# A recurrent-memory attention loop on one core: sums as whole-array matmuls, another order of scores and V, and an output split of 256 + 384 columns

## The chip, the cores and the metric

One core of a Trainium2 chip runs the whole program. The metric is the device time of one execution in microseconds (us); lower is better. TensorE is called PE, its weight loads PEld, VectorE DVE, ScalarE ACT, GpSimd POOL, SyncE SP.

## What is computed

Two attention blocks read the same input x (1 x 2048 x 640, bf16), and a gate mixes them:

```python
g = _sigmoid((x * gate_w).sum(-1, keepdims=True))
a = _A_ref(x, A_mem0, A_Wq, A_Wk, A_Wv, A_Wo, A_seg_len)
b = _B_ref(x, B_wqkv, B_wo)
return g * a + (1 - g) * b
```

Block B is local dilated attention and has no part in the change. Block A goes through x in 64 segments of 32 tokens, one after the other, because each segment's first 8 outputs are the next one's memory:

```python
for s in range(n_seg):
    xs = x[:, s * seg_len:(s + 1) * seg_len, :].copy()
    h = jnp.concatenate([mem, xs], axis=1)            # 8 + 32 rows
    q = jnp.einsum('btd,dhe->bhte', h, Wq)            # 32 heads of 192; k, v alike
    ...
    p = _softmax(scores, axis=-1)                     # scores masked
    o = jnp.einsum('bhqk,bhke->bhqe', p, v)
    o = jnp.einsum('bhte,hed->btd', o, Wo)
    mem = o[:, :M, :].copy()
    outs.append(o[:, M:, :])
```

## The kernel before

Block B runs first (`part_b`), then `prepass` computes, for all segments at once, the projections of eight of a segment's tokens, called z below, and puts them in `zpk_dram`. Then `part_a` runs the 64 segments, here called **rounds**, and `part_z` adds the outputs of the z tokens at the end. The change is in `part_a`, with small consequences in `weights_setup`, `tile_of`, `wo_slice`, `wo_place` and `part_z`.

**Matrices.** A round works on 32 columns: 8 memory rows and 24 of the segment's tokens, in `hT` (640 features in 5 chunks of 128, `kc` = 0 to 4). Each of Wq, Wk, Wv is 640 x 6144, cut into 4 quarters J and in each of these 3 units u of 512 columns. `project` (L768) takes one unit and one chunk: four matmuls of 32 weight columns, one per column group of the array (`tile_position=(0, 32 * j)`), with the four J side by side; such four are called a **pass**. A unit needs five passes.

**Streamed weights.** Most weights stay in SBUF. 14 tiles of 384 KB, listed in `STREAM` (L15), do not fit and come from DRAM in every round, through `get_unit` (L565) into 5 rotating buffers, on SP's queue in the order of use. The output matrix Wo is cut into a column part "oa" and a column part "ob", both in tiles of 1536 columns; before the change "oa" has 384 columns (4 chunks of Wo's rows to a tile) and "ob" 256 (6 chunks to a tile).

**A round**, in the order written out by hand for PE, ACT and DVE under `manual_schedule` (L764); the code is at L959 to L1043:

1. First projections. `m_qk(i, kcs)` is unit i // 2 of Q (i even) or K (i odd). The chunks of `hT` whose memory rows are ready are taken first: `sel("oa")` of the round before has written chunks 0 to 2. Then `sel_b` (L953, L956) fetches the memory rows of the remaining chunks, `tail` (L1048, L1052) and `store` (L1058) finish the output of the round before, and the other passes follow. `c_qk(i)` (L786) is ACT's copy out of PSUM, `t_qk` (L794) the transposes, `c_t` DVE's copies.
2. Scores of the first half of the heads, h = 0: `s_a`, `s_b` (L827, L836). HALF are matmuls on half the array's rows (64), FULL on all 128. `e_exp(0)` on ACT, `e_mask(0)` (L849) on DVE.
3. V: `m_v(u)`, copied by DVE in `c_v(u)` (L883), unit 1 in two halves. Between them stand `e_norm(h)` (L859), the sums of the exponentials as matmuls with the block diagonal of ones `bones`, four 32-column groups for each of two widths (160 and 64); `e_recip_a` (ACT: Ln, Exp), `e_recip_b` (DVE: L871, L872); and the scores and the mask of h = 1.
4. P·V: `pv_half(h)` (L899, L904) for h = 0 after three passes of V's last unit, with the other two behind `e_norm(1)`; `c_x`, `c_z` (L913, L920) copy the results on ACT and DVE.
5. Output: `o_group(part, i2)` (L942), twelve groups of four matmuls for each part; the first six of a part need the first P·V only. The order is six of "oa", `pv_half(1)`, five of "ob", six of "oa", the copy of "oa" (L1032, ACT, to `whi`), seven of "ob" with `sel("oa")` after the fourth, the copy of "ob" (L1040). ACT also issues the DMA of the round's z results (`oz_dram`, L1025) and the load of the next round's z data (`load_z`, L753).

PSUM: `psm` has two banks under one tag, taken in turn; Q's and K's units (but for K's first), V's units and the two output parts use it. `part_z` takes its accumulators from the same pool (L1101), "oa" first, and scales them on DVE (L1110).

Of the kernel before, what the change touches and what calls it, by code (L numbers as in the profile page):

```python
# [11 lines left out]
F32 = mybir.dt.float32  # L12
# [3 lines left out]
          ("v", 2, 2), ("oa", 0), ("ob", 0), ("oa", 5), ("ob", 7))  # L16
# [13 lines left out]
class _K:  # L30
# [466 lines left out]
    def weights_setup(self):  # L497
# [5 lines left out]
        rest += [k for k in [("oa", i) for i in range(12)] + [("ob", i) for i in range(8)] if k not in STREAM]  # L503
# [10 lines left out]
    def tile_of(self, pool, k):  # L514
        n = 1536 if k[0] in ("oa", "ob") else 512 * len(self.units(*k))
        t = pool.tile([128, n], BF, name="w_" + "_".join(map(str, k)))
        self.res_tiles[k] = t if n < 1536 or k[0] in ("q", "k", "v") else t[:].rearrange(
            "p (c f) -> p c f", c=4 if k[0] == "oa" else 6)
        return t
# [13 lines left out]
    def wo_slice(self, k, dst):  # L533

        n, f0, f1 = (4, 0, 384) if k[0] == "oa" else (6, 384, 640)
# [3 lines left out]
    def wo_place(self, part, c):  # L539

        n = 4 if part == "oa" else 6
# [178 lines left out]
    def part_a(self):  # L720
# [4 lines left out]
        with ctx:  # L725
# [22 lines left out]
            psm = ctx.enter_context(tc.tile_pool(name="psm", bufs=2, space=bass.MemoryType.PSUM, reuse_waits="tile"))  # L748
# [16 lines left out]
            for s in range(nseg):  # L765
                pqs, sts, pTs, pSs = {}, {}, {}, {}

                def project(ps, m, u, kcs):  # L768
                    for kc in kcs:
                        st = self.get_unit((m, u, kc)) if (m, u, kc) in STREAM else None  # L770
                        for j in range(4):
                            rhs = self.res(m, j, kc, 512 * u, 512) if st is None or j == 3 else st[:, 512 * j:512 * j + 512]
                            nc.tensor.matmul(ps[32 * j:32 * j + 32, :], lhsT=hT[:, kc, :], rhs=rhs, start=(kc == 0),  # L773
                                             stop=(kc == KC - 1), tile_position=(0, 32 * j), skip_group_check=True)
# [46 lines left out]
                def s_a(R, chunks):  # L821
# [3 lines left out]
                    for t, par, k0, k1 in chunks:  # L825
# [4 lines left out]
                                         start=(r == 0 and t == 1), stop=False, tile_position=(k0, 0),  # L830
                                         skip_group_check=True)

                def s_b(h, chunks):
                    for t, par, k0, k1 in chunks:
# [4 lines left out]
                                         start=False, stop=(t != 1), tile_position=(k0, 0), skip_group_check=True)  # L839
# [12 lines left out]
                def e_norm(h):  # L852
# [3 lines left out]
                    for x, E_x in ((80, EA), (32, EB)):  # L856
                        for j in range(4):
# [69 lines left out]
                def o_group(part, i2):  # L927
                    n = 384 if part == "oa" else 256
                    if i2 == 0:
                        pso[part] = psm.tile([128, 512], F32, tag="m", name="ps_wo")  # L930
                    for jj in range(4):
# [3 lines left out]
                        if (part, i) not in osl:  # L935
# [5 lines left out]
                            osl[part, i] = w[:].rearrange("p (c f) -> p c f", c=4 if part == "oa" else 6)  # L941
# [68 lines left out]
                m_v(2, (0, 1, 2))  # L1010
# [4 lines left out]
                m_v(2, (3, 4)); c_v(2)  # L1015
# [4 lines left out]
                for i2 in range(6):  # L1020
                    o_group("oa", i2)
# [10 lines left out]
                nc.scalar.copy(whi[:, 0:384], pso["oa"][:, 0:384])  # L1032
# [142 lines left out]
```

## Time and profile before

| | us |
|---|---|
| three runs | 1703.22, 1704.7, 1705.23 |
| median of them | 1704.7 |
| the profiled execution | 1702.23 |
| its span, first to last instruction | 1700.5 |
| first and 63rd `tail` matmuls in it | 385.4 and 1616.9 |
| matmuls of `part_z` in it | 1642.0 to 1696.4 |

In a row of the page's groups or of a timeline stand the engine, the line, the operation, what it writes and reads, the shapes and the count; "busy, mean ns of one" and the idle time of the engine just before, with what ended it in brackets. "issue" there means that no semaphore explains the wait. A timeline row begins with its start and its duration in us, and merges neighbours of one kind (x16); the duration of a matmul is that of its whole way through the array, so that successive ones overlap, and their pace is read from the starts. A row of the windows view gives the stretch, its length, the busy time (and count) of PE, PEld, DVE, ACT and POOL, the granted clock of PE, the DMA share and GB/s. PEld is the loading of weights, which runs beside the matmuls. Lines are those of the kernel before.

### The profile page before, as it was taken

The page shows a single profiled execution, that of the slowest core. Times are in us where ns is not written, and L with a number is a line of the kernel's source. Part 1 is how long each engine was busy: PE and PEld are TensorE (multiplying, and loading weights), DVE is VectorE, ACT ScalarE, POOL GpSimd, SP SyncE. Part 2 cuts the span into 40 slices and gives each one's busy share as a digit, 9 for nine tenths or more (in the row PEclk, how much of TensorE's full clock was granted, in tenths as well). Part 3 has the DMA queues.
Part 4 walks back from the last instruction along what each step waited for, and adds up shares of the span by engine and source line. Part 5 has one row for each costly group of instructions (what it writes and reads, how often), then busy time and mean ns, then how long its engine had stood idle before and what let it go on. Part 6 is the DMA issues. An engine that isn't in the chain of part 4 may idle for free.

```text
span 1700.5 us, 75713 instructions
## 1 busy us (share of the span) xinstructions
PE 1600.5 (94%) x33209; PEld 887.1 (52%) x33209; DVE 700.9 (41%) x2223; ACT 804.5 (47%) x2082; POOL 59.8 (4%) x124
## 2 busy tenths in 40 slices
PE   7887999989999999999999999999999999999989
PEld 4544544445555555555555555555555555555559
DVE  3665333234434444443344434434444434444430
ACT  3877422234444444444445444445454444454450
POOL 2030000000000000000000000000000000000000
PEclk9999899999999999999999999999999999999999
DMA  7798798889989999998999989999999999999981
GB/s 202 186 209 216 227 312 232 257 245 305 305 301 311 305 303 313 300 313 288 300 314 313 308 288 309 318 299 320 304 321 306 306 300 304 307 309 309 306 274 31
DMA packets 307608, 479.44 MB, mean 282 GB/s; under 512 B 100556, under 2 KB 186444, under 8 KB 307276
## 3 DMA queue, kind: packets, MB, share of 16 engines
q1 hardware_dynamic: 208144, 418.12, 75.8%
q10 hardware_dynamic: 99132, 56.46, 11.8%
q8 instruction: 260, 4.26, 1.0%
q14 instruction: 72, 0.59, 0.1%
HBM read 432.76 MB, written 47.23 MB: 282 GB/s over the span
## 4 chain that ended last, share of the span: by engine, by line
PE 85%; DMA 6%; ACT 3%; issue 3%; DVE 1%; SPq 1%; ACTq 0%; DVEq 0%
PE ps_qk L773 25%; PE ps_v L773 13%; PE ps_wo L942 13%; PE ps_pre L622 6%; PE ps_qkT L794 5%; PE ps_S L827 5%; PE ps_oT L899 3%; PE ps_z L1106 3%; PE ps_pre L652 3%; DMA wst<-wscr 2%; PE ps_S L859 2%; PE ps_bqk L236 2%; ACT ZB L1032 2%; DMA bqkT<-bqk_dram 1%; PE ps_mem L953 1%
## 5 line engine op out<-in xcount | busy, mean ns | idle before, releaser
L773 PEld LDWEIGHTS <-hT 128*32 128x32 bf16 x11520 | 277.2, 97 | 287.0 <-issue 18.6
L786 ACT CAST TZ<-ps_qk 128x512 bf16<-128x512 f32 x384 | 218.7, 587 | 315.3 <-PE ps_qk L773 315.3
L773 PE MATMUL ps_qk<-w_q,hT 128*32 128x512 bf16 x3264 | 267.9, 383 | 1.8 <-issue 1.6
L773 PE MATMUL ps_qk<-w_k,hT 128*32 128x512 bf16 x3264 | 266.0, 380 | 2.4 <-issue 2.0
L773 PE MATMUL ps_v<-w_v,hT 128*32 128x512 bf16 x3072 | 245.5, 384 | 0.0
L805 DVE COPY ZB<-ps_qkT 128x512 bf16<-128x512 bf16 (+1 forms) x256 | 91.0, 356 | 349.4 <-PE ps_qkT L794 253.7
L942 PEld LDWEIGHTS <-TZ 128*32 128x32 bf16 x6144 | 146.0, 96 | 110.4 <-ACT TZ L913 39.9
L883 DVE CAST TZ<-ps_v 128x512 bf16<-128x512 f32 (+1 forms) x256 | 136.9, 556 | 45.5 <-PE ps_v L773 45.5
L942 PE MATMUL ps_wo<-w_oa,TZ 128*32 128x384 bf16 x2560 | 147.4, 330 | 7.3 <-issue 6.8
L773 PE MATMUL ps_qk<-wst,hT 128*32 128x512 bf16 x1152 | 149.0, 381 | 0.8 <-DMA wst<-wscr 0.8
L913 ACT CAST TZ<-ps_oT 128x192 bf16<-128x192 f32 x256 | 75.9, 322 | 129.7 <-PE ps_oT L904 83.8
L942 PE MATMUL ps_wo<-w_ob,TZ 128*32 128x256 bf16 x2304 | 108.2, 275 | 14.0 <-issue 13.9
L956 DVE CAST hT<-ps_mem 128x24 bf16<-128x24 f32 x126 | 22.5, 179 | 227.6 <-PE ps_mem L953 227.6
L913 DVE CAST TZ<-ps_oT 128x192 bf16<-128x192 f32 x256 | 85.8, 355 | 57.7 <-PE ps_oT L904 55.8
L773 PE MATMUL ps_v<-wst,hT 128*32 128x512 bf16 x768 | 100.7, 387 | 9.0 <-DMA wst<-wscr 8.9
L794 PE MATMUL ps_qkT<-ident,TZ 128*128 128x128 bf16 x1536 | 107.3, 219 | 0.0
L794 PEld LDWEIGHTS <-TZ 128*128 128x128 bf16 x1536 | 88.6, 98 | 26.9 <-issue 26.9
L942 PE MATMUL ps_wo<-wst,TZ 128*32 128x256 bf16 (+1 forms) x1280 | 96.9, 302 | 4.8 <-issue 4.4
L845 ACT ACTIVATE TZ<-ps_S 32x224 bf16<-32x224 f32 x256 | 89.3, 349 | 13.0 <-PE ps_S L836 10.7
L845 ACT ACTIVATE ZB<-ps_S 32x224 bf16<-32x224 f32 x256 | 89.2, 348 | 13.0 <-PE ps_S L836 9.3
L754 POOL COPY TZ<-ZB 128x384 bf16<-128x384 bf16 x64 | 32.5, 507 | 1467.4 <-DMA ZB<-zpk_dram 565.1
L827 PE MATMUL ps_S<-ZB,TZ 64*128 64x160 bf16 (+1 forms) x704 | 78.1, 234 | 0.0
(135 smaller groups left out, 2037.6 us busy)
## 6 DMA issues: line engine op xcount, KB each, us to landing
wst<-wscr SPq DMA_DIRECT2D x896, 384.0 KB
zpk_dram<-ZS ACTq DMA_DIRECT2D x4, 3072.0 KB
ZB<-zpk_dram ACTq DMA_DIRECT2D x64, 192.0 KB
zpk_dram<-ZV ACTq DMA_DIRECT2D x32, 192.0 KB
TZ<-zpk_dram ACTq DMA_DIRECT2D x64, 96.0 KB
oz_dram<-TZ ACTq DMA_DIRECT2D x64, 96.0 KB
w_q<-in_A_Wq_dram SPq DMA_DIRECT2D x14, 384.0 KB
w_k<-in_A_Wk_dram SPq DMA_DIRECT2D x14, 384.0 KB
```

Of the source, the lines that this page charges most:

```text
L622: nc.tensor.matmul(ps[:], lhsT=weights(j, kc, 6 * Rp + 3 * r + t), rhs=zTi[:, kc, :], start=(kc == 0), stop=(kc == KC - 1))
L652: mm = nc.tensor.matmul(pss[g][:], lhsT=zTi[:, kc, 128 * st:128 * st + 128], rhs=weights(kc, g), start=(kc == 0), stop=(kc == KC - 1))
L773: nc.tensor.matmul(ps[32 * j:32 * j + 32, :], lhsT=hT[:, kc, :], rhs=rhs, start=(kc == 0), stop=(kc == KC - 1), tile_position=(0, 32 * j), ...
L786: nc.scalar.copy(sts[i], pqs[i][:])
L794: nc.tensor.transpose(pT[:, 128 * t:128 * t + 128], st[:, 128 * t:128 * t + 128], self.ident[:])
L805: nc.vector.tensor_copy(QTf[:, run[2]:run[2] + 4, run[3]:run[3] + n, :].rearrange("p b x i -> p x b i"), src.rearrange("p (x b i) -> p x b ...
L827: nc.tensor.matmul(grid(h, par)[:, :, 0:80].rearrange("p j (b r i) -> p j b r i", r=2, i=8)[:, :, :, r, :], lhsT=KTs[3 * R + t][k0:k1, :], ...
L845: nc.scalar.activation(E[ps], pSs[h][ps, :, 112 * j:112 * j + 112], ACT.Exp, scale=scale_a)
L883: nc.vector.tensor_copy(VU[u][:, f0:f1], pvs[u][:, f0:f1])
L899: nc.tensor.matmul(out[:, r, t, :], lhsT=Vt[6 * h + 3 * r + f0 // 128][ks, f0 % 128:f0 % 128 + f1 - f0], rhs=E[ks, par, 0:80].rearrange("p ...
L913: cp(oTxs[2 * h + j // 2][:, 6 * (j % 2):6 * (j % 2) + 6, :], pos[j][:, 0:240].rearrange("p (c q) -> p c q", q=40)[:, :, 8:40])
L942: nc.tensor.matmul(pso[part][32 * jj:32 * jj + 32, 0:n], lhsT=oTxs[2 * (g // 2) + J // 2][:, 6 * (J % 2) + 3 * (g % 2) + t, :], rhs=osl[pa ...
```

## The change

- **Output split.** "oa" becomes columns 0 to 255 (6 chunks to a tile, 8 tiles), "ob" columns 256 to 639 (4 chunks to a tile, 12 tiles). The streamed output tiles become ob 0, oa 0, oa 7 and ob 5.
- **Order of the output.** Six groups of "ob", the second P·V, all twelve of "oa", its copy (256 columns), six of "ob" with `sel("oa")` after the fourth of them, the copy of "ob" (384 columns). `sel("oa")` now brings chunks 0 and 1 of the next `hT`, `sel_b` chunks 2 to 4.
- **Order of the first projections.** Ahead of `sel_b`: chunks 0 and 1 of `m_qk(0)` and of `m_qk(1)` and chunk 0 of `m_qk(2)`; one pass of `m_qk(2)` instead of `m_qk(1)` between `sel_b` and `tail`; then chunks 2 to 4 of each. `start` and `stop` of a unit go by count, since chunks don't all come in the same order. The two `psm` banks get a tag each, so that Q's second unit can be open beside Q's first.
- **First sums.** For h = 0, `e_norm` is one matmul of the whole array for each width, two instead of eight.
- **Second scores.** For h = 1 FULL comes ahead of HALF.
- **V.** Two passes of V's last unit stand ahead of the first P·V instead of three, three behind `e_norm(1)` instead of two.

The diff, cut to its core:

```diff
 
 STREAM = (("k", 0, 2), ("q", 1, 1), ("k", 1, 2), ("q", 2, 1), ("q", 2, 4), ("k", 2, 4), ("v", 0, 0), ("v", 1, 0), ("v", 1, 3),
-          ("v", 2, 2), ("oa", 0), ("ob", 0), ("oa", 5), ("ob", 7))
+          ("v", 2, 2), ("ob", 0), ("oa", 0), ("oa", 7), ("ob", 5))
 ...
-        n, f0, f1 = (4, 0, 384) if k[0] == "oa" else (6, 384, 640)
+        n, f0, f1 = (6, 0, 256) if k[0] == "oa" else (4, 256, 640)
 ...
             for s in range(nseg):
                 pqs, sts, pTs, pSs = {}, {}, {}, {}
 
+                def bank(n, name):
+                    return psm.tile([128, 512], F32, tag="mn"[(s + n) % 2], name=name)
+
+                done = {}
+
                 def project(ps, m, u, kcs):
                     for kc in kcs:
+                        n = done[m, u] = done.get((m, u), 0) + 1
                         st = self.get_unit((m, u, kc)) if (m, u, kc) in STREAM else None
                         for j in range(4):
                             rhs = self.res(m, j, kc, 512 * u, 512) if st is None or j == 3 else st[:, 512 * j:512 * j + 512]
-                            nc.tensor.matmul(ps[32 * j:32 * j + 32, :], lhsT=hT[:, kc, :], rhs=rhs, start=(kc == 0),
-                                             stop=(kc == KC - 1), tile_position=(0, 32 * j), skip_group_check=True)
+                            nc.tensor.matmul(ps[32 * j:32 * j + 32, :], lhsT=hT[:, kc, :], rhs=rhs, start=(n == 1),
+                                             stop=(n == KC), tile_position=(0, 32 * j), skip_group_check=True)
 
                 def m_qk(i, kcs):
                     if i not in pqs:
                         pqs[i] = psS.tile([128, 2, 512], F32, tag="S", name="ps_qk")[:, 0, :] if i == 1 else \
-                            psm.tile([128, 512], F32, tag="m", name="ps_qk")
 ...
-                                         start=(r == 0 and t == 1), stop=False, tile_position=(k0, 0),
+                                         start=(r == 0 and (t == 1) == (h == 0)), stop=False, tile_position=(k0, 0),
 ...
                     pz = pSs[h][:, 0, 0:160].rearrange("p (a f) -> p a f", a=2)
                     for x, E_x in ((80, EA), (32, EB)):
+                        if h == 0:
+                            nc.tensor.matmul(pz[:, :, 0:x], lhsT=self.bones[:], rhs=E_x, start=(x == 80), stop=(x == 32))
+                            continue
 ...
-                        pvs[u] = psm.tile([128, 512], F32, tag="m", name="ps_v")
+                        pvs[u] = bank(u != 1, "ps_v")
 ...
-                    m0, m1 = (0, 3) if part == "oa" else (3, KC)
+                    m0, m1 = (0, 2) if part == "oa" else (2, KC)
 ...
-                m_qk(0, (0, 1, 2))
+                m_qk(0, (0, 1))
                 m_qk(1, (0, 1))
+                m_qk(2, (0,))
                 if sel_b is not None:
                     sel_b()
-                m_qk(1, (2,))
+                m_qk(2, (1,))
                 if tail is not None:
                     tail()
-                m_qk(0, (3, 4)); c_qk(0)
-                m_qk(1, (3, 4)); c_qk(1)
+                m_qk(0, (2, 3, 4)); c_qk(0)
+                m_qk(1, (2, 3, 4)); c_qk(1)
                 if store is not None:
                     store()
-                m_qk(2, range(KC)); c_qk(2)
+                m_qk(2, (2, 3, 4)); c_qk(2)
                 m_qk(3, range(KC)); c_qk(3)
                 m_qk(4, (0, 1))
 ...
                 e_norm(0); e_recip_a(0); e_recip_b(0)
+                s_a(2, FULL); s_a(3, FULL); s_b(1, FULL)
                 s_a(2, HALF); s_a(3, HALF); s_b(1, HALF)
-                s_a(2, FULL); s_a(3, FULL); s_b(1, FULL)
                 e_exp(1)
                 m_v(1, (1, 2, 3, 4)); c_v(1)
                 e_mask(1)
-                m_v(2, (0, 1, 2))
+                m_v(2, (0, 1))
                 pos = pv_half(0)
                 c_x(0, pos, (0, 1, 3), "add")
                 e_norm(1)
                 e_recip_a(1)
-                m_v(2, (3, 4)); c_v(2)
+                m_v(2, (2, 3, 4)); c_v(2)
                 e_recip_b(1)
                 c_x(0, pos, (2,), "a")
                 c_z(0, pos, (1, 3), "aa")
                 c_z(0, pos, (0, 2), "dd")
                 for i2 in range(6):
-                    o_group("oa", i2)
+                    o_group("ob", i2)
                 pos = pv_half(1)
                 c_x(1, pos, range(4), "adda")
                 c_z(1, pos, range(4), "adad")
                 nc.scalar.dma_start(self.oz_dram[s], zst)
                 if s + 1 == nseg:
                     self.sort_oz(0)
-                for i2 in range(5):
-                    o_group("ob", i2)
-                for i2 in range(6, 12):
+                for i2 in range(12):
                     o_group("oa", i2)
-                nc.scalar.copy(whi[:, 0:384], pso["oa"][:, 0:384])
+                nc.scalar.copy(whi[:, 0:256], pso["oa"][:, 0:256])
                 if s + 1 < nseg:
                     load_z(s + 1)
                     pm = psS.tile([128, 2, 512], F32, tag="S", name="ps_mem")
-                for i2 in range(5, 12):
+                for i2 in range(6, 12):
                     o_group("ob", i2)
-                    if i2 == 8 and s + 1 < nseg:
+                    if i2 == 9 and s + 1 < nseg:
                         sel("oa", hT_next, pm)
-                nc.scalar.copy(whi[:, 384:640], pso["ob"][:, 0:256])
+                nc.scalar.copy(whi[:, 256:640], pso["ob"][:, 0:384])
                 if s + 1 < nseg:
 ...
-            for part, f0, nf in (("oa", 0, 384), ("ob", 384, 256)):
-                ps = psm.tile([128, 512], F32, tag="m", name="ps_z")
+            for part, f0, nf in (("oa", 0, 256), ("ob", 256, 384)):
+                ps = psm.tile([128, 512], F32, tag="m" if f0 else "n", name="ps_z")
```

More of the change, by code (lines that the diff above doesn't have):

```diff
@@ L502, in weights_setup @@
             rest += [(m, J, kc) for kc in ks for J in range(4)]
-        rest += [k for k in [("oa", i) for i in range(12)] + [("ob", i) for i in range(8)] if k not in STREAM]
+        rest += [k for k in [("oa", i) for i in range(8)] + [("ob", i) for i in range(12)] if k not in STREAM]
         n = (0, N_EARLY, -N_MID - N_V - N_LAST, -N_V - N_LAST, -N_LAST, None)
@@ L517, in tile_of @@
         self.res_tiles[k] = t if n < 1536 or k[0] in ("q", "k", "v") else t[:].rearrange(
[L518 removed]
+            "p (c f) -> p c f", c=6 if k[0] == "oa" else 4)
         return t
@@ L539, in wo_place @@
     def wo_place(self, part, c):
-        n = 4 if part == "oa" else 6
+        n = 6 if part == "oa" else 4
         return c // n, c % n
@@ L778, in m_qk @@
                         pqs[i] = psS.tile([128, 2, 512], F32, tag="S", name="ps_qk")[:, 0, :] if i == 1 else \
-                            psm.tile([128, 512], F32, tag="m", name="ps_qk")
+                            bank(i == 2 or i == 4, "ps_qk")
                     project(pqs[i], ("q", "k")[i % 2], i // 2, kcs)
@@ L927, in o_group @@
                 def o_group(part, i2):
-                    n = 384 if part == "oa" else 256
+                    n = 256 if part == "oa" else 384
                     if i2 == 0:
-                        pso[part] = psm.tile([128, 512], F32, tag="m", name="ps_wo")
+                        pso[part] = bank(part == "oa", "ps_wo")
                     for jj in range(4):
```

6 lines of the change are left out of this document (3 added, 3 removed).

## The prediction

> **What bounds the kernel now.** I read the page first, then the span between two marks of the loop, then PE's waits, then one loop round in order of time. From the page, the shares of engines, the chain that ended last, and the queue that brings PE its instructions:
>
> ```profile
> PE 1600.5 (94%) x33209; PEld 887.1 (52%) x33209; DVE 700.9 (41%) x2223; ACT 804.5 (47%) x2082; POOL 59.8 (4%) x124
> PE 85%; DMA 6%; ACT 3%; issue 3%; DVE 1%; SPq 1%; ACTq 0%; DVEq 0%
> L786 ACT CAST TZ<-ps_qk 128x512 bf16<-128x512 f32 x384 | 218.7, 587 | 315.3 <-PE ps_qk L773 315.3
> q8 instruction: 260, 4.26, 1.0%
> ```
>
> PE is the bound: 94% busy, 85% of the chain. So a change pays only by what it takes out of PE's own line of work, or out of a wait that stops PE. The groups by line, cut to the stretch 385 to 1617 us and to the line of `tail`, give the length of a round (four matmuls each):
>
> ```profile
> L1048 PE MATMUL ps_a<-ZB,sel_x x252: 232/233/233, 385.4 to 1616.9; 128*32 128x160 bf16 x126
> ```
>
> 252 / 4 = 63 rounds begin between 385.4 and 1616.9, 62 intervals, 19.86 us each. One without a pause, 1064.62 to 1083.68, takes 19.06 (PE and PEld rows mixed with DVE and ACT, start, duration; an LDWEIGHTS row in brackets tells who let PE go on):
>
> ```profile
> 1064.62 0.24 PE L1048 MATMUL ps_a<-ZB,sel_x 128*32 128x160 bf16 x4
> ...
> 1073.47 0.39 PE L773 MATMUL ps_v<-wst,hT 128*32 128x512 bf16 x3
> 1073.51 0.27 DVE L849 TENSOR_TENSOR TZ<-TZ,mask 128x224 bf16<-128x224 bf16 x1 [0.19 <-ACT TZ L845]
> 1073.83 0.28 PE L859 MATMUL ps_S<-TZ,bones 128*32 128x160 bf16 x8
> 1074.05 0.24 PE L827 MATMUL ps_S<-ZB 64*128 64x160 bf16 x2
> 1074.35 0.24 PE L827 MATMUL ps_S<-ZB 128*128 128x160 bf16 x1
> 1074.43 0.30 PE L827 MATMUL ps_S<-ZB,TZ 128*128 128x160 bf16 x2
> 1074.63 0.27 PE L836 MATMUL ps_S<-ZB,TZ 128*128 128x128 bf16 x2
> 1074.84 0.61 PE L773 MATMUL ps_v<-w_v,hT 128*32 128x512 bf16 x8
> 1075.94 0.76 DVE L883 CAST TZ<-ps_v 128x256 bf16<-128x256 f32 x2 [0.62 <-PE ps_v L773]
> 1076.46 0.17 PEld L899 LDWEIGHTS <-TZ 32*128 32x128 bf16 x16 [0.42 <-DVE TZ L883]
> 1076.61 0.26 DVE L849 TENSOR_TENSOR ZB<-ZB,mask 128x224 bf16<-128x224 bf16 x1
> 1076.93 0.28 PE L859 MATMUL ps_S<-ZB,bones 128*32 128x160 bf16 x8
> 1077.04 0.60 PE L773 MATMUL ps_v<-w_v,hT 128*32 128x512 bf16 x8
> 1077.53 0.35 PE L942 MATMUL ps_wo<-wst,TZ 128*32 128x384 bf16 x4
> 1077.70 0.69 DVE L883 CAST TZ<-ps_v 128x512 bf16<-128x512 f32 x1
> 1078.80 0.17 PEld L899 LDWEIGHTS <-TZ 32*128 32x128 bf16 x16 [0.40 <-DVE ZB L872]
> 1079.27 0.40 PE L942 MATMUL ps_wo<-wst,TZ 128*32 128x256 bf16 x6
> 1080.37 0.66 PE L942 MATMUL ps_wo<-w_oa,TZ 128*32 128x384 bf16 x12
> 1080.58 0.35 ACTq L1025 DMA_DIRECT2D oz_dram<-TZ  x1
> 1080.86 0.61 PE L942 MATMUL ps_wo<-w_ob,TZ 128*32 128x256 bf16 x16
> 1081.08 0.48 ACT L1032 CAST ZB<-ps_wo 128x384 bf16<-128x384 f32 x1 [0.54 <-PE ps_wo L942]
> 1081.61 0.14 PEld L953 LDWEIGHTS <-ZB 128*128 128x128 bf16 x3 [0.43 <-ACT ZB L1032]
> 1081.78 0.39 PE L942 MATMUL ps_wo<-wst,TZ 128*32 128x256 bf16 x6
> 1081.89 0.18 DVE L956 CAST hT<-ps_mem 128x24 bf16<-128x24 f32 x1 [1.44 <-PE ps_mem L953]
> 1082.12 0.77 PEld L773 LDWEIGHTS <-hT 128*32 128x32 bf16 x20
> 1082.34 0.37 ACT L1040 CAST ZB<-ps_wo 128x256 bf16<-128x256 f32 x1 [0.78 <-PE ps_wo L942]
> 1083.32 0.11 PEld L953 LDWEIGHTS <-ZB 128*128 128x128 bf16 x2 [0.42 <-issue]
> 1083.68 0.24 PE L1048 MATMUL ps_a<-ZB,sel_x 128*32 128x160 bf16 x4
> ```
>
> Four waits of PE lie in it: for the first mask (L859, 1073.83), the V copy (1076.46), the second normalisation (1078.80) and the copy of the first output part (1081.61). The other 0.80 us of a mean round are single pauses of up to 2 us that no semaphore ends ("issue"), mostly in the output stage:
>
> ```profile
> PE ps_wo L942 <- issue: 23.9, 25, 1.9
> PE ps_qk L773 <- DMA wst<-wscr: 0.3, 1, 0.3
> 981.93 0.62 PE L942 MATMUL ps_wo<-w_ob,TZ 128*32 128x256 bf16 x16 [1.94 <-issue]
> 983.30:986.20 2.90, 2.90 (x38) 0.97 (x34) 0.17 (x1) 0.37 (x1) 0.51 (x1) 0.52 0.58 188
> ```
>
> I read them as PE's instructions coming late: 4.26 MB came in 260 packets, 16 KB each, and 2 x 33209 instructions make 64 bytes each, so 256 to a packet; the output and P·V stages use them up fastest. Streamed weights are late just once (0.3 us). The last row shows a pause's second price: after 1.94 us of idling the granted clock of the stretch 983.3 to 986.2 is 0.52, and 38 matmuls run in 2.9 us.
>
> **Prices.** A pass is four matmuls in the four column groups. Seven passes of 512 columns lie from 1074.84 to 1076.46, 1.62; with 0.09 for the change of array shape that is 0.219 a pass. Three of 384 columns: 1080.37 to 1080.86, 0.164. Three of 256: 1081.78 to 1082.12, 0.11. The change of shape: the two L836 at 1074.63 stream 2 x 128 columns, 0.11, yet the next begins at 1074.84: 0.10 left over. PE's end to a copy's start is 0.22 (1080.86 to 1081.08), a copy's end to PE 0.05.
>
> **Step 1, first sums and second scores.** Eight sums in column groups become two of the whole array; 64 x 12 PE instructions go. Before: 1073.83 to 1074.05, 0.22, of which 0.10 is the change to half arrays. The new form stands in no row. By columns 160 + 64 cost 0.10; by the nearest rows, whole-array matmuls of 160 columns from 1074.35 to 1074.43, two cost 0.16. I take 0.13. The whole-array scores follow without a change of shape, so full (0.49 with one change) and half (0.30 with one) cost as now: 0.22 becomes 0.13, **-0.09**. The new change ahead of the sums is free while the mask covers it: the last pass starts at 1073.47, its successor could at 1073.69, the mask ends at 1073.78, and the sums start at 1073.83, so 0.14 of waiting covers 0.10. If it doesn't, the step saves nothing.
>
> The Trainium skill, "TensorEngine Tiling (Array Packing)", Key Properties, says that changing the tiling mode drains TensorE, while another tile of the same mode does not. Counted by that alone the edit gains nothing, six microseconds less in the sum: three changes from one V pass to the next before, three after. The trace's 0.10 agrees that a change costs something, and its 0.14 wait is why I count one as free.
>
> **Step 2, a V pass moved behind P·V.** `m_v(1)` begins at 1074.75 and its copy 1.10 later as now, 1075.85; the first half takes about 0.42 (0.76 for two that overlap), so 1076.27, and P·V may use it at 1076.32. With six passes instead of seven PE is there at 1076.15: 0.17 of the 0.22 moved becomes a wait for DVE (P·V's first matmuls read the older V tile, but what they win ends at the next gate). DVE's second mask follows that copy, 1076.78, so the second sums go at 1076.84 (-0.09). Three passes instead of two then end at 1077.61; the V copy starts 0.22 later, at 1077.83 instead of 1077.70, and DVE's chain from it to the second P·V (1077.70 to 1078.80, 1.10) stays: 1078.93, **+0.13**. PE would be ready at 1077.61 + 0.98 + 0.10 = 1078.69, so more passes there cover nothing.
>
> **Step 3, output split.** 48 x 384 and 48 x 256 columns stay; only order and cover change. P·V ends at 1079.40 (0.47 later, as now). Twelve groups of 256 end at 1080.71 and the copy, now 256 columns (0.37), could start at 1080.93. But on ACT's queue ahead of it stands the store of oz (1080.58 to 1080.93, waiting for copies of P·V), now 0.13 later, to 1081.06. Copy 1081.08 to 1081.45, `sel` at 1081.50 instead of 1081.62. PE itself is ready at 1080.71 + 0.66 + 0.10 = 1081.47: four groups of 384 cover what four of 256 didn't. After it two matmuls and two groups of 384, 0.13 + 0.33, or the hT cast, some 0.24 + 0.18 + 0.05: projection at 1081.97 instead of 1082.12, **-0.15**.
>
> **Step 4, first projections.** Still five passes between, but `sel_b` has three matmuls: +0.03. ACT copies of 0.59 now come after 3, 6 and 9 passes (0.66 apart) instead of 2, 4 and 9; both orders put 16 passes ahead of the transposes, so nothing. SP asks for streamed units in the order of use, each when the fifth before it is released; ("q",1,1) now takes the place of ("k",0,2) and comes no later than that did. The copy of the last part is 0.48 long and must also free the bank for Q's second block at the fifth pass, 1081.97 + 0.88 = 1082.85; it ends near 1082.66, 0.2 ahead. A round: **-0.12**, times 63 = -7.
>
> **Step 5, the rest.** Pauses for instructions: 12 fewer of some 890 a round take 1% of 50 us, -0.5; the output stretch gets denser and the V stretch thinner, so 0 to me, bounds -4 to +6. Lost cover (the 0.2 for the bank when a ZB load holds ACT's queue; streamed units closer together): +1. At the end, part Z:
>
> ```profile
> 1642.70 0.47 ACT L1032 CAST ZB<-ps_wo 128x384 bf16<-128x384 f32 x1
> 1643.22 0.83 PE L1106 MATMUL ps_z<-wst,w_q 128*32 128x384 bf16 x16 [0.88 <-ACT ZB L1032]
> ```
>
> Its first bank is now freed by the second copy, not the first: +0.4. Sum: -7 - 0.5 + 1 + 0.4 = -6. The profiled execution took 1702.2 (span 1700.5 and 1.7 around it), so 1696; the runs' median is 1704.7, 2.5 above, and I forecast for the median: **1698.5**.
>
> **Rivals.**
> 1. The gain is eaten (0.20): the change of shape isn't hidden and the moved pass costs all its 0.22 at the second P·V. For: that wait is DVE's already. Against: the 0.14. A round: +0.22 at 1079.02, `sel` at 1081.59, -0.03 + 0.03 = 0; the median stays at 1704 to 1706.
> 2. The copy isn't held by the store, and the second V copy waits less (0.08): `sel` at 1081.30 to 1081.47, -0.2 to -0.3 a round, 1687 to 1692. For: engines' queues may run ahead. Against: 1080.58 + 0.35 fits closely before 1081.08.
> 3. Slower, by streamed weights (0.07). The last streamed unit of the output (the 256-column one at 1081.78) becomes a 384-column one at 1080.71 + 0.33 = 1081.04, 0.74 earlier, while its slot is free only 0.09 earlier. If units land in the last 0.65 us before their use, PE waits there: from 0.18 us a round on the kernel is slower (1708), at 0.65 it is 1739. Against: just one wait of 0.3 in 62 rounds. No row shows when a unit lands.
> 4. More instruction pauses (0.10): `sel` to the next projection has the same instructions in 0.28 less, so pauses that end there (25 now) grow by that, +7, and each that passes 2 us adds some 1.5 at half clock: 1702 to 1711.
>
> The Trainium skill, "Runtime: NRT & Kernel Launch", Instruction fetch mechanics, says that the sequencer fetches 256 instructions at a time during execution and that this is mostly hidden. By that rule rival 4 and my -0.5 would be nothing. The 1.94 us pause that no semaphore ended speaks against it here.
>
> **How the numbers follow.** Forecast (steps 1 to 4 as worked out, 1695 to 1701) 0.55; rivals as given. About 0.2%, 3.4 us, is what can be told from no change: below 1701.3 is faster, above 1708.1 slower. Faster: 0.55 + 0.08 = 0.63. Same: 0.20 and half of rival 4, 0.05, is 0.25. Slower: 0.07 and the other half is 0.12. The range, 1689 to 1707, leaves out rival 3's long part and the ends of 2 and 4.
>
> **What would show it.** In a round without pauses: 18.94 us from `tail` to `tail`; sums to scores 0.13; whole-array scores at once after them; P·V's first half stopped by L892's V copy; second P·V 0.13 later against the mask; `sel` let go by ACT, the oz store ending just before its copy; instruction pauses near 0.8 us a round. Wrong if the sums take 0.2, if DMA ends waits at the new output units, or if pauses pass 1 us a round.

## The result, and the profile after it

| | before | after |
|---|---|---|
| median of the runs, us | 1704.97 (4 runs, 1703.22 to 1711.09) | **1682.77** (4 runs, 1678.37 to 1684.86) |
| ratio after / before | | 0.9856, 95% interval 0.9829 to 0.9882 |
| the profiled execution, us | 1702.23 | 1683.8 |
| first `tail` | 385.4 | 380.2 |
| 62 rounds, first to 63rd `tail` | 1231.5 | 1216.3 |
| the shortest round | 19.06 | 18.92 |
| pauses in a mean round | 0.81 | 0.70 |
| last part, from the 63rd `tail` to the end of the span | 83.5 | 85.5 |

The kernel is faster by 1.4%, 22 us. The sign was forecast, the size was not: 1698.5 was expected, and the result lies below the range of 1689 to 1707. In this table and below, the **clean round** is the 3rd percentile of the 62 distances from one first `tail` matmul to the next (the shortest lie within 0.01 us of each other), and the pauses are the mean distance less that. So the 18.4 us between the two profiled executions are 5.2 ahead of the first `tail` (the first round is among them), 62 x 0.14 = 8.8 in clean rounds, 62 x 0.10 = 6.4 in pauses, and 2 given back from the 63rd `tail` on.

Lines shift by 6 to 9 in the changed kernel: `project` is L779, the copies of Q and K L792, the first sums L864, the scores L833 and L842, the V copy L892, P·V L908 and L913, the output L951, `sel` L962, its cast L965, the two output copies L1040 and L1048, `tail` L1056. From the page of the changed kernel, the engines, the chain, the Q and K copies and PE's instruction queue:

```profile
PE 1583.4 (94%) x32809; PEld 908.9 (54%) x32825; DVE 704.8 (42%) x2223; ACT 812.9 (48%) x2082; POOL 59.8 (4%) x124
PE 77%; DMA 10%; DVE 5%; issue 4%; ACT 2%; ACTq 1%; SPq 0%; DVEq 0%
L792 ACT CAST TZ<-ps_qk 128x512 bf16<-128x512 f32 x384 | 224.6, 585 | 309.9 <-PE ps_qk L779 299.4
q8 instruction: 257, 4.21, 1.0%
```

PE is still the bound, with 94% of a span that is 18.5 us shorter. The first and the last row belong together: by the code 64 x 6 matmuls and as many loads are gone, and 3 packets of 16 KB with them. (The counts fall by 400 and 384: this trace lacks the records of 16 matmuls of `prepass`.)

Next, one round of the changed kernel without a pause, from the timeline (start, duration, and in brackets the idle time and what ended it). It runs from `tail` at 1361.85 to `tail` at 1380.77:

```profile
1361.85 0.24 PE L1056 MATMUL ps_a<-ZB,sel_x 128*32 128x160 bf16 x4
...
1371.06 0.26 PE L864 MATMUL ps_S<-TZ,bones 128*128 128x160 bf16 x2
1371.16 0.23 PE L833 MATMUL ps_S<-ZB 128*128 128x160 bf16 x1
...
1371.64 0.10 PEld L833 LDWEIGHTS <-ZB 64*128 64x128 bf16 x2
...
1371.94 0.61 PE L779 MATMUL ps_v<-w_v,hT 128*32 128x512 bf16 x8
...
1373.04 0.76 DVE L892 CAST TZ<-ps_v 128x256 bf16<-128x256 f32 x2 [0.53 <-PE ps_v L779]
1373.35 0.27 PEld L908 LDWEIGHTS <-TZ 32*128 32x128 bf16 x16 [0.42 <-issue]
...
1373.71 0.27 DVE L855 TENSOR_TENSOR ZB<-ZB,mask 128x224 bf16<-128x224 bf16 x1
...
1374.03 0.28 PE L868 MATMUL ps_S<-ZB,bones 128*32 128x160 bf16 x8
...
1375.01 0.69 DVE L892 CAST TZ<-ps_v 128x512 bf16<-128x512 f32 x1 [0.28 <-PE ps_v L779]
...
1376.11 0.17 PEld L908 LDWEIGHTS <-TZ 32*128 32x128 bf16 x16 [0.56 <-DVE ZB L881]
...
1377.89 0.35 ACTq L1035 DMA_DIRECT2D oz_dram<-TZ  x1
...
1378.29 0.37 ACT L1040 CAST ZB<-ps_wo 128x256 bf16<-128x256 f32 x1 [0.43 <-PE ps_wo L951]
...
1378.71 0.11 PEld L962 LDWEIGHTS <-ZB 128*128 128x128 bf16 x2 [0.37 <-ACT ZB L1040]
...
1379.18 0.86 PEld L779 LDWEIGHTS <-hT 128*32 128x32 bf16 x20 [0.22 <-DVE hT L965]
...
1380.38 0.14 PEld L962 LDWEIGHTS <-ZB 128*128 128x128 bf16 x3 [0.34 <-issue]
...
1380.77 0.24 PE L1056 MATMUL ps_a<-ZB,sel_x 128*32 128x160 bf16 x4
```

To compare it with the round of before, take off the start of each (1361.85 here, 1064.62 there):

| us from `tail` | before | forecast | after |
|---|---|---|---|
| first sums | 9.21 | 9.21 | 9.21 |
| first scores behind them | 9.43 | 9.34 | 9.31 |
| V passes | 10.22 | 10.13 | 10.09 |
| first P·V | 11.84 | 11.70 | 11.50 |
| second sums | 12.31 | 12.22 | 12.18 |
| second P·V | 14.18 | 14.31 | 14.26 |
| `sel` | 16.99 | 16.88 | 16.86 |
| next projection | 17.50 | 17.35 | 17.33 |
| next `tail` | 19.06 | 18.94 | 18.92 |

This is the part of the forecast that held. What did not lies between such rounds. PE's waits, from the first `tail` to the 63rd (total us, times, longest):

```profile
PE ps_oT L908 <- DVE ZB L881: 11.1, 62, 0.2
PE ps_wo L951 <- issue: 10.7, 17, 1.3
PE ps_qk L779 <- issue: 6.4, 7, 1.9
PE ps_qk L779 <- ACT ZB L1048: 3.8, 5, 1.1
PE ps_qk L779 <- DMA wst<-wscr: 1.4, 2, 1.2
```

Before, the output's pauses, which nothing but "issue" ends, came to 23.9 us in 25 places; now it is 10.7 in 17. These rows count idle time from the moment the last matmul has left the array, so they give less than what the pace loses (the pause of 1.94 us that the prediction shows is 2.26 from start to start).

### The profile page after: what moved, and what is told of

The parts are those of the page before. It is cut to its first block, busy times and chain, and to the rows that moved or that the text cites. A ratio compares the mean times of both kernels' runs of the same rounds, so it can differ in the third digit from the quotient of the medians.

```text
span 1682.0 us, 74929 instructions
## 1 busy us (share of the span) xinstructions
PE 1583.4 (94%) x32809; PEld 908.9 (54%) x32825; DVE 704.8 (42%) x2223; ACT 812.9 (48%) x2082; POOL 59.8 (4%) x124
## 4 chain that ended last, share of the span: by engine, by line
PE 77%; DMA 10%; DVE 5%; issue 4%; ACT 2%; ACTq 1%; SPq 0%; DVEq 0%
PE ps_qk L779 25%; PE ps_v L779 11%; PE ps_wo L951 9%; PE ps_pre L622 6%; DMA wst<-wscr 5%; PE ps_qkT L800 5%; PE ps_S L833 4%; PE ps_z L1114 3%; PE ps_pre L652 3%; PE ps_oT L908 2%; DVE TZ L892 2%; DMA bqkT<-bqk_dram 2%; PE ps_bqk L236 1%; PE ps_S L842 1%; DVE ZB L880 1%
## 5 line engine op out<-in xcount | busy, mean ns | idle before, releaser
L779 PEld LDWEIGHTS <-hT 128*32 128x32 bf16 x11520 | 285.2, 96 | 299.5 <-issue 30.2
L792 ACT CAST TZ<-ps_qk 128x512 bf16<-128x512 f32 x384 | 224.6, 585 | 309.9 <-PE ps_qk L779 299.4
L779 PE MATMUL ps_qk<-w_q,hT 128*32 128x512 bf16 x3264 | 287.3, 383 | 5.6 <-ACT ZB L1048 3.8
L779 PE MATMUL ps_qk<-w_k,hT 128*32 128x512 bf16 x3264 | 252.9, 379 | 5.3 <-issue 4.9
L779 PE MATMUL ps_v<-w_v,hT 128*32 128x512 bf16 x3072 | 244.2, 384 | 0.0
L951 PEld LDWEIGHTS <-TZ 128*32 128x32 bf16 x6144 | 161.5, 96 | 52.3 <-issue 20.4
L892 DVE CAST TZ<-ps_v 128x512 bf16<-128x512 f32 (+1 forms) x256 | 136.9, 556 | 58.2 <-PE ps_v L779 58.0
L951 PE MATMUL ps_wo<-w_ob,TZ 128*32 128x384 bf16 x2560 | 153.3, 327 | 2.1 <-issue 2.0
L779 PE MATMUL ps_qk<-wst,hT 128*32 128x512 bf16 x1152 | 150.7, 382 | 1.4 <-DMA wst<-wscr 1.4
L779 PE MATMUL ps_v<-wst,hT 128*32 128x512 bf16 x768 | 101.4, 386 | 8.8 <-DMA wst<-wscr 8.8
L965 DVE CAST hT<-ps_mem 128x16 bf16<-128x16 f32 x126 | 22.5, 179 | 202.7 <-PE ps_mem L962 202.7
L951 PE MATMUL ps_wo<-w_oa,TZ 128*32 128x256 bf16 x2304 | 92.0, 273 | 7.8 <-issue 7.8
L951 PE MATMUL ps_wo<-wst,TZ 128*32 128x256 bf16 (+1 forms) x1280 | 97.1, 297 | 2.2 <-issue 2.2
L908 PEld LDWEIGHTS <-TZ 32*128 32x128 bf16 (+1 forms) x4096 | 47.1, 97 | 72.1 <-DVE ZB L881 36.1
```

Of the source, the lines that this page charges most:

```text
L792: nc.scalar.copy(sts[i], pqs[i][:])
L892: nc.vector.tensor_copy(VU[u][:, f0:f1], pvs[u][:, f0:f1])
L908: nc.tensor.matmul(out[:, r, t, :], lhsT=Vt[6 * h + 3 * r + f0 // 128][ks, f0 % 128:f0 % 128 + f1 - f0], rhs=E[ks, par, 0:80].rearrange("p ...
L951: nc.tensor.matmul(pso[part][32 * jj:32 * jj + 32, 0:n], lhsT=oTxs[2 * (g // 2) + J // 2][:, 6 * (J % 2) + 3 * (g % 2) + t, :], rhs=osl[pa ...
```

## The experiments

Two accounts were open. The first, that of the prediction: the change pays by its clean round, pauses are a toll that stays. The second: the V pass behind P·V thins out PE's instructions just where they come late, so step 2, counted as a loss, is what pays. Each kernel below was run beside the kernel before on the same chip; e1 to e4 share one, e5 to e8 another, e9 to e12 a third. "Pauses" and "clean" are as above and come from the one profiled execution of each.

### Undoing one part each

e1 puts the V pass back:

```diff
-                m_v(2, (0, 1))
+                m_v(2, (0, 1, 2))
 ...
-                m_v(2, (2, 3, 4)); c_v(2)
+                m_v(2, (3, 4)); c_v(2)
```

> The changed kernel with three V passes ahead of the first P.V again and two behind it (step 2 undone). Theory A, the schedule of PE's waits as worked out in the prediction: the moved pass costs 0.13 to 0.2 us a round, so without it the round without pauses falls from the changed kernel's 18.92 to 18.7 to 18.8 us, and the kernel is 8 to 12 us faster than the changed one if pauses stay at 0.70 us a round. Rival B, the moved pass thins PE's instructions where they are used fastest: the round without pauses falls as in A, but pauses grow to 0.9 or more a round and the time is that of the changed kernel or above.

e2 puts the first sums back into eight matmuls, and HALF ahead of FULL:

```diff
-                        if h == 0:
-                            nc.tensor.matmul(pz[:, :, 0:x], lhsT=self.bones[:], rhs=E_x, start=(x == 80), stop=(x == 32))
-                            continue
 ...
+                s_a(2, HALF); s_a(3, HALF); s_b(1, HALF)
                 s_a(2, FULL); s_a(3, FULL); s_b(1, FULL)
-                s_a(2, HALF); s_a(3, HALF); s_b(1, HALF)
```

> The changed kernel with eight sums in column groups and half-array scores first again (step 1 undone). Theory A: the round without pauses is 19.0 us instead of 18.92, so 5 to 6 us slower than the changed kernel. Rival B, fewer PE instructions mean fewer pauses: beside the 0.09, pauses go back from 0.70 to 0.80 us a round, and the kernel is 11 to 13 us slower than the changed one.

e3 has both of these edits: what is left is the output split with the first projections.

> The output split of 256 + 384 with its order and the new first projections alone; steps 1 and 2 undone. Theory A: the copy of the first part waits for PE or for ACT's oz store at 16.33 us into the round, sel starts near 16.75, and the round without pauses is 18.8 us (19.06 before, 18.92 after): with pauses as before, 0.80, the kernel is 15 us faster than before. Rival B, pauses depend on the density of PE's instructions and grow: 0.9 to 1.1 a round, and the kernel gains 5 us or less.

e4 is the changed kernel again, with no edit.

> The changed kernel unchanged, to see what differs from one execution to the next. Theory A, the part ahead of the loop (4.3 us shorter in the first profile, although its instructions are the same) and the pauses vary from execution to execution: the round without pauses is 18.92 again, the start of the loop differs by some us, pauses between 0.6 and 0.8 a round. Rival B, both belong to the change: the first tail again near 380 us and pauses at 0.70 within 0.03.

| | median us (runs) | ratio to before, 95% | clean | pauses |
|---|---|---|---|---|
| e1, V pass back | 1689.72 (12) | 0.9940, 0.9910 to 0.9970 | 18.71 | 1.01 |
| e2, sums back | 1687.76 (6) | 0.9921, 0.9892 to 0.9949 | 19.05 | 0.58 |
| e3, split alone | 1699.13 (12) | 0.9974, 0.9951 to 0.9997 | 18.84 | 0.98 |
| e4, changed again | 1682.58 (6) | 0.9885, 0.9853 to 0.9917 | 18.92 | 0.74 |

The clean rounds add up: the split takes 0.22 off (19.06 to 18.84), the sums 0.13 (18.84 to 18.71, and 19.05 to 18.92), and the moved pass adds 0.20 or 0.21 (18.71 to 18.92, 18.84 to 19.05). Yet the version with the shortest clean round, e1, is 7 us slower than e4. Its waits, then those of e2, then the largest of e3, over the 62 rounds:

```profile
PE ps_wo L951 <- issue: 32.9, 34, 1.8
PE ps_qk L779 <- issue: 3.0, 6, 1.1
```

```profile
PE ps_wo L948 <- issue: 12.1, 20, 1.2
PE ps_oT L905 <- DVE ZB L878: 11.2, 62, 0.2
```

```profile
PE ps_wo L948 <- issue: 29.6, 30, 1.9
```

With the pass ahead of P·V the output loses 32.9 us in 34 pauses (e1) and 29.6 in 30 (e3); with it behind, 12.1 in 20 (e2), 10.7 in 17 and, in e4, 14.7 in 21. In place of them stands a wait for DVE of 0.18 in each of the 62 rounds, 11.2 in all. The first account is refuted here: the moved pass costs 0.20 of a clean round and saves 0.27 to 0.40 of pauses. And the split by itself adds pauses, 0.98 against 0.81, which takes most of its 0.22 back: e3 is hardly faster than before. Undoing the sums (e2) costs 5 us against e4 and brings no pauses back.

### A second trace of the kernel before

> The kernel before, unchanged, for a second trace of it. Two readings of the 5 us by which the changed kernels reached the first tail earlier (380.2 to 382.8 us in four traces, 385.4 us in the one trace of before). If that belongs to the change, this trace has its first tail at 385 again; if it is how one execution differs from another, it lies at 381 to 383. In both: clean round (the 3rd percentile of the 62 lengths tail to tail) 19.06 us, 892 PE instructions in it, pauses 0.75 to 0.9 us a round.

It took 1705.6 us in the median (12 runs; ratio to the kernel before 1.0003, 0.9977 to 1.0030), clean round 19.06, pauses 0.83. Its first `tail` and the largest wait:

```profile
L1048 PE MATMUL ps_a<-ZB,sel_x x252: 232/233/233, 383.4 to 1616.4; 128*32 128x160 bf16 x126
PE ps_wo L942 <- issue: 24.2, 27, 1.6
```

So the pauses of before repeat. The first `tail` does not: 383.4 here, 385.4 in the first trace, against 380.2 to 382.8 in the five traces of e1 to e4 and the changed kernel. In later runs of versions of it, it is at 383.2 to 384.3 (e10 to e12). The two sets overlap, so I do not count the 5 us to the change but for about one: the last matmul of `prepass`, ahead of the first round, starts at 356.9 and 355.0 in the two traces of before and at 352.6 to 357.7 in those of the changed kernel and its versions, and in the first round PE then waits 5.6 and 5.3 us for a streamed tile of V before (5.1 in e9, which has the old split) and 4.2 to 4.6 with the new split.

### The same kernels without streamed weights

If the pauses are PE waiting for instructions that stand behind weights in the DMA engines, they must go when the loop streams nothing. In e6 (the kernel before), e7 (the changed one) and e8 (the changed one with the V pass back) `get_unit` returns one of five tiles loaded once, so the loop leaves the streaming out and multiplies by these five tiles where it would take the streamed ones:

```diff
         if key in self.ahead:
-            return self.ahead.pop(key)
+            return self.ahead[key]
+        if len(self.ahead) == WBUFS:
+            return self.ahead[STREAM[STREAM.index(key) % WBUFS]]
```

> The kernel before, in which the loop loads no streamed weights: five tiles are loaded once and used again in turn, so projections and output multiply by wrong weights of the right size, and the queues carry about 300 GB/s less in the loop. Theory (PE's pauses come when it uses up 256 instructions faster than the next 16 KB of them arrive between the weights): the pauses fall from 0.81 to under 0.2 us a round, the clean round stays 19.06, the whole takes 1645 to 1660 us. Rival (the pauses are inside PE, whatever the queues do): 0.7 to 0.9 a round as before, 1700 us.

> The same edit to the changed kernel: no streamed weights in the loop, wrong weights in their place. Theory: pauses fall from 0.70 to under 0.2 us a round, the clean round stays 18.92, the whole 8 to 12 us under the kernel before without stream, which is what the clean round alone gives (62 x 0.14 = 8.7). Rival: pauses stay at 0.7.

> The same edit, and the V pass back ahead of P.V (step 2 undone). With the stream this version was slower than the changed kernel by 7 us, with a clean round 0.20 us shorter and pauses 0.27 to 0.3 longer. Theory (the moved pass pays only by parting the instructions, so that the fetch keeps up): without the stream the order turns over, clean round 18.71 and pauses under 0.2, and the whole is 10 to 13 us FASTER than the changed kernel without stream. Rival (the moved pass helps by something else, such as the copies' order or the exchange of PSUM banks): it stays slower by 4 to 8 us.

| | median us (6 runs each) | ratio to before, 95% | clean | pauses |
|---|---|---|---|---|
| e6, before | 1640.06 | 0.9619, 0.9584 to 0.9653 | 19.05 | 0.04 |
| e7, changed | 1633.71 | 0.9582, 0.9551 to 0.9613 | 18.88 | 0.10 |
| e8, changed, V pass back | 1619.47 | 0.9494, 0.9464 to 0.9525 | 18.67 | 0.08 |

The order turns over: with the stream the changed kernel beats the version with the pass put back by 7 us, without it that version is 14 us ahead, 62 x 0.21 = 13 of it from the clean round. Two times came out beside what was expected: e6 is 5 us under its range, and e7 is 6 us ahead of e6 instead of 8 to 12. The windows view of 600 to 1500 us for the changed kernel with the stream and then for e7 (busy us of PE, PEld, DVE, ACT and POOL, PE's clock, share of the DMA engines, GB/s), and last the waits of e6, e7 and e8 for instructions at the output, over their 62 rounds:

```profile
600.00:1500.00 900.00, 866.65 (x20134) 499.63 (x20135) 387.52 (x1380) 451.04 (x1284) 22.86 (x46) 1.00 0.94 310
```

```profile
600.00:1500.00 900.00, 887.33 (x20838) 511.53 (x20834) 397.97 (x1421) 466.75 (x1325) 24.36 (x48) 1.00 0.12 31
```

```profile
PE ps_wo L944 <- issue: 0.8, 2, 0.6
PE ps_wo L953 <- issue: 0.7, 4, 0.2
PE ps_wo L953 <- issue: 0.4, 1, 0.4
```

The DMA share falls from 0.94 to 0.12, and e1's 32.9 us of pauses become 0.4, with the same matmuls in the same order. So the pauses need both: busy DMA engines and a dense stretch of PE's instructions.

### Counting instructions

Two more things tie them to the instruction queue. First, number PE's instructions on record from the start: matmuls, loads, and the 142 semaphore and drain instructions among them. Then 43 of e1's 48 gaps above 0.6 us in the loop (from start to start) end at a number that leaves 177 when divided by 256; in the changed kernel 29 of 34, in e4 30 of 32, and in the kernel before 36 of 37 leave 193 (in e5 41 of 44). The difference of 16 is that of the 16 missing records. Second, PE goes on 1.4 us (median) after a q8 packet has ended. From PE's passing such a number to the end of the next packet it takes about 2.8 us (2.75 to 2.78, medians of the traces of before, after, e1 and e2; 2.62 to 2.88 with those of e3 to e5 and e9 to e12). Read as the time from asking for a block to its coming, 2.8 + 1.4 is 4.2 us: 256 instructions used up in less leave PE waiting. That gives a count that needs only a clean round: for each instruction the time to the 256th after it, what this lacks of 4.2, the mean of that times the blocks a round (892 or 880 / 256).

| | shortest 256, us | pauses counted | measured |
|---|---|---|---|
| before (two traces) | 2.64 | 0.74 | 0.81, 0.83 |
| e3, split alone | 2.64 | 0.90 | 0.98 |
| e1, split and sums | 2.65 | 0.89 | 1.01 |
| e2, split and V pass | 2.96 | 0.71 | 0.58 |
| changed (two traces) | 2.96 | 0.71 | 0.70, 0.74 |

It parts the kernels with many pauses from those with fewer, but not e2 from the changed kernel, and it was made after these runs.

The kernels without the stream agree with it. There the time from such a number (193, since none of the 16 records is missing) to the packet's end is 1.6 us in the median, though the packet's own transfer takes 1.1, no less than with the stream. With 1.6 + 1.4 = 3.0 in place of 4.2 (the 1.4 is taken over) the count gives 0.04, 0.00 and 0.04 us a round for e6 to e8, where 0.04, 0.10 and 0.08 were measured. So what the busy DMA engines lengthen is mainly the wait ahead of the packet's transfer.

The next four kernels test the count.

e9 is the kernel before with step 1 alone; e10 the changed kernel with the second sums on the whole array too (`if h == 0:` becomes `if True:` in `e_norm`); e11 the changed kernel with `m_v(2, (0,))` ahead of P·V and `m_v(2, (1, 2, 3, 4))` behind; e12 has the edits of e10 and e11.

> The kernel before with step 1 alone (first sums in 2 full matmuls, first half of the second scores' order turned; split and V pass as before). Count made from the clean rounds seen so far: for each PE instruction of a round the time to the 256th after it; where that is under 4.2 us, what it lacks; the mean of this times the blocks of 256 in a round. It gives 0.74 for before, 0.71 for the changed kernel, 0.89 and 0.90 with the V pass put back and for the split alone, 0.71 with the sums put back (measured 0.81 and 0.83, 0.70 and 0.74, 1.01, 0.98, 0.58). Step 1 takes its 12 instructions away at 9.2 us of the round, where 256 instructions still take 4.4 us, so the pauses should hardly move: clean round 18.93 to 18.96, pauses 0.75 to 0.85, 1694 to 1699 us. Rival (the earlier gain comes back as pauses): pauses 0.9 to 1.0, 1703 us.

> The changed kernel with the second sums too in 2 matmuls of the whole array: 868 PE instructions a round, 12 fewer at 12.06 us of the round, inside the stretch in which 256 instructions take only 3.1 to 3.7 us. Clean round: sums 0.09 shorter, but they now stand between two passes in strips, with a change of shape (0.10) on either side instead of one: 18.90 to 19.00. Theory (pauses are a matter of instructions in that stretch): pauses fall by 0.08 to 0.15 to 0.58 to 0.65, the whole 1675 to 1683 us. Rival (the number of instructions is not what decides): pauses stay 0.70 to 0.74, whole 1682 to 1687.

> The changed kernel with one more V pass moved behind P.V (one ahead, four behind). Clean round: 0.20 to 0.25 longer again (19.12 to 19.17), as the first moved pass cost 0.20. Theory: the first P.V already lies in a stretch that takes 3.1 us for 256 instructions because of the second P.V, so a pass more between the two widens it to 3.3: pauses fall by 0.1 to 0.2, to 0.5 to 0.6; whole 1683 to 1690 us, no faster than the changed kernel. Rival (each moved pass takes 0.3 of pauses away): pauses 0.4, whole 1676 us.

> Both of the last two edits: all sums by the whole array, one V pass ahead of P.V and four behind. Clean round 19.10 to 19.25, pauses 0.4 to 0.5 by the theory, whole 1678 to 1688 us; if the two gains in pauses do not add, 0.55 and 1688 us. (The label says undo_vpass; the kernel moves the pass further instead.)

| | median us (runs) | ratio to before, 95% | clean | pauses | counted afterwards |
|---|---|---|---|---|---|
| e9 | 1697.65 (12) | 0.9973, 0.9948 to 0.9999 | 18.93 | 1.00 | 0.74 |
| e10 | 1677.89 (6) | 0.9876, 0.9840 to 0.9912 | 19.01 | 0.45 | 0.57 |
| e11 | 1683.43 (6) | 0.9892, 0.9862 to 0.9921 | 19.13 | 0.50 | 0.60 |
| e12 | 1682.32 (6) | 0.9892, 0.9870 to 0.9914 | 19.22 | 0.28 | 0.48 |

Largest waits for instructions in e10 and in e12:

```profile
PE ps_wo L951 <- issue: 6.1, 13, 0.8
PE ps_qk L779 <- issue: 3.6, 7, 1.2
```

```profile
PE ps_qk L779 <- issue: 3.8, 7, 1.1
PE ps_wo L951 <- issue: 1.6, 4, 0.7
```

The direction was right in e10 to e12: 12 instructions fewer in the dense stretch, or a pass more between the two P·V, and the pauses fall, in e12 from the changed kernel's 10.7 us at the output to 1.6. In e11 the clean round grows by as much as the pauses fall (0.21 against 0.20 to 0.24); e10 and e12 keep something (0.09 against 0.25 to 0.29, 0.31 against 0.42 to 0.46). e9 missed: time as expected, pauses 1.00 in place of 0.75 to 0.85. Its profiled execution (1705.4) is 7.8 us above the median of its runs, 0.13 a round if all of it is pauses, which leaves 0.87. The same correction takes e4 from 0.74 to 0.63 and e2 from 0.58 to 0.63, and makes the moved pass worth 0.30 to 0.36 of pauses. The count is no more than a ranking: where it falls, the measured pauses fall by about twice as much, probably because the fetch time is not one number (the middle half of the times to the packet's end is 2.3 to 3.4 us). That reason was not tested.

No version is shown to be faster than the changed kernel. e10 has the lowest median, but its ratio to before, 0.9876, is that of e4, 0.9885, within their intervals.

## Why the prediction was right in sign and wrong in size

- **Step 1 (sums, order of scores)** forecast -0.09 a round; the runs show -0.13 (before to e9; e3 to e1). Two whole-array sums cost 0.10 and not 0.13 (1371.06 to 1371.16), and the change of shape ahead of them is hidden, as said: the sums start at 9.21 as before.
- **Step 2 (V pass behind P·V)** in the clean round: +0.13 at the second P·V although step 1 had won 0.09, so 0.22 for the pass; measured 0.20 to 0.21. P·V's first half isn't stopped by the V copy (11.50, not 11.70), but the next gate, DVE's mask, makes this equal, as its bracket said.
- **Steps 3 and 4 (split, first projections)**: from 14.31 at the second P·V to 18.94 at `tail`, 4.63 against 4.88 before, -0.25; measured -0.22 (before to e3). The oz store ends at 1378.24, the copy that it holds starts at 1378.29: it does wait on ACT's queue. The bracket of its row names PE, but PE had gone on to "ob" 0.39 us earlier, at 1377.90, where 0.22 was enough before.
- The sum of steps 1 to 4, a clean round of 18.94, came out at 18.92. (-0.12 times 63 is -7.6; the prediction's sum has -7.)
- **Step 5 is the one that failed**: "Pauses for instructions: ... -0.5; the output stretch gets denser and the V stretch thinner, so 0 to me, bounds -4 to +6". Both halves of that sentence are real and neither is small. The split alone adds 0.15 to 0.18 a round, some 10 us (e3 against the two traces of before); the moved pass takes away 0.27 to 0.40, 17 to 25 us (e1 against the changed kernel's two traces, e3 against e2). The net is -6.4 us between the first two traces. With it the profiled times differ by 18.4, of which the 5.2 ahead of the first `tail` are, but for about 1, how one execution differs from another. The medians differ by 22, of which clean rounds explain 8.8; that leaves 13, or 15 with the 2 given back at the end, for the pauses and the first round. A profile shows one execution, and runs of one kernel with the stream spread by 6 to 24 us, so the term lies between -6 and about -15 and can't be put closer than this. With -6.4 in the sum the forecast would have been 1692.6, still 10 above the measured median.
- The error behind it: I read the pauses rightly as instructions coming late, and then priced them by the number of instructions in the kernel (1% fewer, 1% of 50 us). What goes with the pauses is how fast PE uses up 256 instructions in the dense stretch (the shortest 256 take 2.64 us before and 2.96 after, and e1, with 2.65, has as many instructions as the changed kernel), and the density could have been counted in the clean round of the trace of before. Even so counted, the net of the change would have been 0.74 to 0.71, some -2 us: right in sign, but the size of the net is explained only in part.
- **Lost cover** was forecast at +1. The bank that the second Q unit needs does cost PE 3.8 us in this trace, by the mechanism named (a ZB load on ACT's queue); in the other seven traces with the new split and the stream it is 0 to 2.9:

```profile
1358.22 2.33 ACTq L753 DMA_DIRECT2D ZB<-zpk_dram  x1
1360.60 0.48 ACT L1048 CAST ZB<-ps_wo 128x384 bf16<-128x384 f32 x1 [2.01 <-issue]
1361.13 0.40 PE L779 MATMUL ps_qk<-w_q,hT 128*32 128x512 bf16 x4 [0.85 <-ACT ZB L1048]
```

  The issue takes 2.33 us where it took 0.42 twenty microseconds later; PE is let go 0.85 late. Each of the five waits of this kind in the trace follows such an issue, of 1.54 to 2.54 us.
- **The end** was forecast at +0.4. From the 63rd `tail` on it takes 83.5, 84.7 and 83.6 us in the traces with the old split (before, e5, e9) and 83.3 to 86.8 in those with the new one: too close to tell.
- **Rivals.** Rival 1 (gain eaten) and rival 2 (copy not held) did not happen. Rival 3 (streamed weights late) neither: 1.4 us of such waits in 62 rounds. Rival 4 (more instruction pauses) is true of the split, at about the size it gave (+7), and was outweighed by the pass that the prediction held to be a pure loss. Its second price is small: the loop has one record of half clock, 3.41 us long, in the changed kernel's trace (three in e4), two in that of before (none in e5). A rival "fewer pauses by the moved pass", with a price and a chance, was missing.
- The Trainium skill, "Runtime: NRT & Kernel Launch", Instruction fetch mechanics, calls the fetch mostly hidden. That agrees with e6 to e8 (0.04 to 0.10 us a round at a DMA share of 0.12) and not with the kernel as it runs (0.7 to 1.0 us at 0.94).

## What to carry to other kernels

Where a kernel keeps the DMA engines as busy as here (0.94) and PE runs many small matmuls, look for PE's "issue" waits, find the stretch in which 256 matmuls and loads take the least time, and put long matmuls inside it, as the moved pass does. An instruction is then dear or cheap by where it stands, and an order that is shorter in every undisturbed round may be the slower one, as e1 was. Price such pauses by the density at their place and not by the total count.

## What the runs showed of the hardware that was not expected

- PE's instructions come 256 at a time, and their coming can stop PE: "issue" waits add up to 34 us of the loop before and some 42 in e1, by a mere exchange of passes, and to less than 1 in each kernel without streamed weights. The pauses as a whole are 50, 62 and 3 to 6 us.
- PE goes on about 1.4 us after the packet has ended, and the packet ends 2.8 us after PE passes the mark, while its own transfer takes 0.97 us (medians). Most of the delay is not the transfer, and it is this part that shrinks without the stream (2.8 to 1.6 us).
- An ACT DMA issue, the load of the z data, takes 0.42 us in the median of 64 in the changed kernel's trace, but over 1 us in 19 of them and up to 2.54; the long ones kept ACT's next copy, and with it PE, waiting.
